# Batch 0 of an attention and MoE kernel by other routes: half of q and k by two more queues in fp32, v first, global keys by a one-hot matmul, masks on VectorE

## The chip, the cores and the metric

The kernel runs on one core of one Trainium2 chip. The metric is the device time of one execution in microseconds (us); smaller is better.

Engine names as in the profile: PE is the TensorE matmul, DVE is VectorE, ACT is ScalarE, POOL is GpSimd, SP is SyncE. A name with a `q` behind it (`SPq`) is that engine's sequencer issuing a DMA.

## The reference, cut to what matters

```python
batch, n_heads, seq, head_dim = (8, 8, 576, 64)      # q, k, v in fp32; n_global = 8
scores = (1/sqrt(D)) * q @ k.T
mask = abs(pos_i - pos_j) <= 32                      # a band of 65 keys ...
mask = mask | is_global[:, None] | is_global[None,:] # ... plus 8 global rows and columns
attn = softmax(where(mask, scores, -1e9)) @ v
x = attn.transpose(0, 2, 1, 3).reshape(4608, 512)
h = x @ w_in                                         # first layer, 512 x 2048
g = h + sin(alpha * h)**2 / (alpha + 1e-9)
out = g @ w_out                                      # second layer, 2048 x 512
```

## The kernel before

The 4608 tokens go through the two layers in nine chunks of 512. Chunk `p` holds the tokens that the attention of batch `p` has just finished, so the program is a pipeline: attention of batch 0 alone (the prologue), then first layer of chunk 0, then second layer of chunk 0 interleaved with the attention of batch 1, and so on. In the prologue the big matrix products have nothing to do. Data for the attention come in by three queues: GpSimd's (with a cast from fp32 to bf16 on the way), SP's and ACT's.

```python
# order of the prologue in the kernel before
zero_v(0); zero(Kps)                       # VectorE, two memsets of about 2.6 us among them
ld0 = load_slots(0, True)                  # GpSimd: cast loads of k, q by head, and of v
for f in ld0[:4]: f()                      # k, q of heads 0 and 1
...                                        # some 20 small GpSimd operations: the masks
for f in ld0[4:]: f()                      # v, then k, q of heads 2 to 7
for i, src in enumerate((k, q, v)):        # the 8 global rows of all 8 batches,
    for eng, js in halves:                 # half by SP, half by ScalarE; each DMA's address
        for j in js:                       # comes from a register that holds the index
            eng.dma_start(out=gN[i][j::NG], in_=src[:, :, bass.ds(regs[j], 1), :])
nc.scalar.dma_start(out=alphaT[:], in_=moe_alpha.rearrange("(t p) -> p t", p=P))
...                                        # masks on VectorE
stage_T(0, 0, psA, "qp")                   # transposes of k, q, heads 0 and 1
globals_all()                              # cast gN[0], gN[1] to gB; transposes into GT
...
globals_v_all()                            # VgN <- gN[2] (cast); recipT <- 1/alpha
shift_v(0); global_v(0)                    # SP: v shifted by half a window; VgN stored into VW
parts, last = attention(0, psA, {2: 0, 3: 2})
with_extra(parts, w_loads, 3, 2)           # GpSimd: w_in, w_out (four quarters each)
parts[3] = partial(chain, parts[3], pool_regs)
late = load_slots(1, True)                 # batch 1, issued inside chunk 0's first layer
```

A step of the attention is the scores (`Sp`), the exponential (`E`) times a mask, the denominators (`den`), and the value matmul (`num`), which reads `VW`: the window's rows of v, and at partitions 112 to 119 the global rows of v. These arrive by the longest path in the prologue: gather to `gN`, cast to `VgN`, then a store from SBUF to SBUF into `VW` (`VW<-VgN`). The outputs of global queries are scattered last, by eight register-addressed copies on GpSimd (`xT<-xg`); the first layer waits for those.

The softmax here doesn't subtract the row's maximum and nothing guards it: scores larger than these inputs give would overflow.

Of the kernel before, what the change touches and what calls it, by code (L numbers as in the profile page):

```python
# [18 lines left out]
def kernel(  # L19
# [12 lines left out]
    P = 128  # L32
# [99 lines left out]

    setup = tc.alloc_tile_pool(name="setup", bufs=1)
# [8 lines left out]
    nc.scalar.dma_start(out=gcol[KB : KB + NG, :], in_=global_idx[:, None])  # L142
    nc.scalar.preload_act_table_set("natural_log_exp_and_others")
# [4 lines left out]
    def zero_v(i):  # L148
        zero(VW[i][96:128].rearrange("p a u n -> p (a u n)").bitcast(F32))
        zero(VW[i][0:32, 0, 0, :].bitcast(F32))  # L150
        zero(VW[i][64:128, 1, NU - 1, :].bitcast(F32))

    zero_v(0)
    zero(Kps[:].bitcast(F32))

    ld0 = load_slots(0, True)
    for f in ld0[:4]:
        f()
    make_identity(nc, identb[:])


    MB = setup.tile([P, 3, QB], F32, name="MB")
    MG = setup.tile([P, NG], F32, name="MG")
    nc.gpsimd.memset(MB[:], 1.0)
    nc.gpsimd.memset(MG[:], 1.0)
    for base, cm, st_ in ((0, 1, -1), (2 * WIN, -1, 1)):
        nc.gpsimd.affine_select(
            out=MB[:], in_=MB[:], compare_op=ALU.is_ge, fill=0.0,
            base=base, channel_multiplier=cm, pattern=[[0, 3], [st_, QB]],
        )  # L170

    for i, base, cm in ((0, -WIN, 1), (2, S - 1 + WIN - (NW - 1) * QB, -1)):
        nc.gpsimd.affine_select(
            out=MB[:, i], in_=MB[:, i], compare_op=ALU.is_ge, fill=0.0,
            base=base, channel_multiplier=cm, pattern=[[0, QB]],
        )

    for base, cm in ((-WIN, 1), (WIN + QB - 1, -1)):
        nc.gpsimd.affine_select(
            out=MG[:], in_=MG[:], compare_op=ALU.is_ge, fill=0.0,  # L180
            base=base, channel_multiplier=cm, pattern=[[0, NG]],
        )

    RF = setup.tile([P, 1 + NG], F32, name="RF")
    nc.gpsimd.memset(RF[:], 1.0)
    for base, cm in ((-KB, 1), (KB + NG - 1, -1)):
        nc.gpsimd.affine_select(
            out=RF[:, 0:1], in_=RF[:, 0:1], compare_op=ALU.is_ge, fill=0.0,
            base=base, channel_multiplier=cm, pattern=[[0, 1]],
        )  # L190
    nc.gpsimd.affine_select(
        out=RF[:, 1:], in_=RF[:, 1:], compare_op=ALU.is_ge, fill=0.0,
        base=-KB - 1, channel_multiplier=1, pattern=[[-1, NG]],
    )
    IQi = setup.tile([P, S], DT.int32, name="IQi")
    nc.gpsimd.iota(IQi[:], pattern=[[1, S]], base=0, channel_multiplier=0)
    for f in ld0[4:]:
        f()

    for hp in range(NHP):  # L200
        zero(kTw[hp][:, :, KB:P])
    zero_v(1)
    nc.vector.memset(ones[:], 1.0)

    gN = [setup.tile([NG * B, DM], F32, name=f"gN{i}") for i in range(3)]
    halves = ((nc.sync, range(0, NG // 2)), (nc.scalar, range(NG // 2, NG)))
    regs = {}
    for eng, js in halves:
        for j in js:
            regs[j] = eng.value_load(  # L210
                gsc[0:1, 2 * j : 2 * j + 1], min_val=0, max_val=S - 1
            )
    for i, src in enumerate((k, q, v)):
        for eng, js in halves:
            for j in js:
                eng.dma_start(
                    out=gN[i][j : NG * B : NG, :].rearrange("b (h d) -> b h d", d=D),
                    in_=src[:, :, bass.ds(regs[j], 1), :].rearrange("b h o d -> b h (o d)"),
                )
    nc.scalar.dma_start(out=alphaT[:], in_=moe_alpha.rearrange("(t p) -> p t", p=P))  # L220

    Gf = setup.tile([P, NG], F32, name="Gf")
    nc.vector.tensor_copy(out=Gf[:], in_=gall[:].bitcast(DT.int32)[:, 0::2])
    Gp = setup.tile([P, 1], F32, name="Gp")
    nc.vector.tensor_copy(out=Gp[:], in_=gcol[:].bitcast(DT.int32)[:, 0:1])


    EQ = setup.tile([P, NG], F32, name="EQ")
    nc.vector.scalar_tensor_tensor(
        out=EQ[:], in0=Gf[:], scalar=Gp[:, 0:1], in1=RF[:, 1:],  # L230
        op0=ALU.is_equal, op1=ALU.mult,
    )
    flag = setup.tile([P, 1], F32, name="flag")
    nc.vector.tensor_reduce(out=flag[:], in_=EQ[:], axis=mybir.AxisListType.X, op=ALU.max)
    nc.vector.tensor_scalar(
        out=flag[:], in0=flag[:], scalar1=-1.0, scalar2=1.0, op0=ALU.mult, op1=ALU.add
    )
    nc.vector.tensor_tensor(out=flag[:], in0=flag[:], in1=RF[:, 0:1], op=ALU.mult)
    DQ = setup.tile([P, S], F32, name="DQ")
    nc.vector.tensor_copy(out=DQ[:], in_=IQi[:])  # L240
    nc.vector.tensor_scalar(
        out=DQ[:], in0=DQ[:], scalar1=Gp[:, 0:1], scalar2=None, op0=ALU.subtract
    )
    nc.vector.tensor_tensor(out=DQ[:], in0=DQ[:], in1=DQ[:], op=ALU.mult)
    nc.vector.tensor_scalar(
        out=DQ[:], in0=DQ[:], scalar1=float(WIN * WIN), scalar2=flag[:, 0:1],
        op0=ALU.is_gt, op1=ALU.mult,
    )
    DQv = DQ[:].rearrange("p (i c) -> p i c", c=QB)
# [305 lines left out]
    for p in range(NCH):  # L555
        fill = []
        late = []
        if p < B:
            with phase_pool("psA", 1) as psA:
                if p == 0:  # L560
                    stage_T(0, 0, psA, "qp")
                    globals_all()
                    for hp in range(NHP):
                        globals_in(0, hp, nc.vector)
# [94 lines left out]
```

## Time and profile before

The median is 386.33 us (385.18 to 386.82, three runs); the profiled run's span is 385.0 us. TensorE is busy for 87% of it.

From chunk 1 on TensorE has hardly a gap: about 38.4 us per chunk. So a change to the prologue is read in the timeline up to chunk 1's first layer. The columns are start, duration, engine, source line, operation, output and inputs, shapes, count; the bracket says how long the engine had been idle and what ended that.

```profile
11.51 3.99 ACTq L216 DMA_DIRECT2D gN<-in_v_dram  x4
...
20.42 0.81 SPq L127 DMA_DIRECT2D VW<-VgN  x1
...
22.03 0.73 ACT L342 ACTIVATE E<-Sp 128x672 bf16<-128x672 f32 x1
...
25.36 0.25 DVE L279 RECIPROCAL recipT<-alphaT 128x16 f32<-128x16 f32 x1 [4.96 <-DMA alphaT<-in_moe_alpha_dram]
...
29.27 0.58 PE L375 MATMUL num<-E,VW 128*64 128x56 bf16 x12 [2.36 <-DMA VW<-VgN]
...
46.29 16.56 PE L457 MATMUL hb<-xT,w_in 128*128 128x512 bf16 x64 [3.36 <-POOL xT L402]
62.69 1.89 PE L494 MATMUL ops<-w_out,H2b 128*128 128x512 bf16 x8
...
90.68 9.67 PE L457 MATMUL hb<-xT,w_in 128*128 128x512 bf16 x44 [1.46 <-POOL xT L402]
```

The reader is to see four milestones: first exponential 22.03, first value matmul 29.27 (it waits for the store of the global rows of v), first layer of chunk 0 at 46.29, lasting to the second layer's start at 62.69, and first layer of chunk 1 at 90.68.

### The profile page before, as it was taken

The page shows a single profiled execution, that of the slowest core. Times are in us where ns is not written, and L with a number is a line of the kernel's source. Part 1 is how long each engine was busy: PE and PEld are TensorE (multiplying, and loading weights), DVE is VectorE, ACT ScalarE, POOL GpSimd, SP SyncE. Part 2 cuts the span into 40 slices and gives each one's busy share as a digit, 9 for nine tenths or more (in the row PEclk, how much of TensorE's full clock was granted, in tenths as well). Part 3 has the DMA queues.
Part 4 walks back from the last instruction along what each step waited for, and adds up shares of the span by engine and source line. Part 5 has one row for each costly group of instructions (what it writes and reads, how often), then busy time and mean ns, then how long its engine had stood idle before and what let it go on. Part 6 is the DMA issues. An engine that isn't in the chain of part 4 may idle for free.

```text
span 385.0 us, 8609 instructions
## 1 busy us (share of the span) xinstructions
PE 336.2 (87%) x3208; PEld 162.9 (42%) x3208; DVE 244.9 (64%) x551; ACT 258.4 (67%) x435; POOL 249.3 (65%) x394
## 2 busy tenths in 40 slices
PE   1128499798999999999999999999999999999796
PEld 0015244443444444444544444444444444344342
DVE  7725459574977497649774976497749774954500
ACT  1057487786988588858885888578857885744310
POOL 8934396227878589858986898689768006854400
PEclk9999999999999999999999999999999999999989
DMA  6999999257999409940994099409940001000012
GB/s 53 136 162 161 190 164 165 37 77 77 155 132 153 124 9 103 148 127 7 103 148 126 7 103 149 128 6 113 137 128 5 30 30 54 2 28 27 29 54 82
DMA packets 133723, 35.31 MB, mean 92 GB/s; under 512 B 123314, under 2 KB 128178, under 8 KB 133682
## 3 DMA queue, kind: packets, MB, share of 16 engines
q0 software_dynamic: 122560, 19.02, 69.4%
q1 hardware_dynamic: 8034, 15.54, 13.9%
q10 hardware_dynamic: 3088, 0.21, 0.8%
q8 instruction: 25, 0.41, 0.4%
q14 instruction: 16, 0.13, 0.1%
HBM read 38.42 MB, written 9.44 MB: 124 GB/s over the span
## 4 chain that ended last, share of the span: by engine, by line
PE 52%; ACT 18%; DVE 10%; issue 7%; POOL 7%; DMA 3%; POOLq 1%; ACTq 0%; DVEq 0%
PE hb L457 22%; PE ops L494 13%; PE o L494 8%; ACT Sb L464 6%; ACT E L342 4%; DMA KS<-in_k_dram 3%; DVE H2b L447 3%; PE num L375 3%; ACT S L470 2%; DVE S L472 2%; DVE kTw L310 2%; ACT lnd L358 2%; PE hb L494 2%; ACT rec L360 2%; PE Sp L336 2%
## 5 line engine op out<-in xcount | busy, mean ns | idle before, releaser
L457 PE MATMUL hb<-xT,w_in 128*128 128x512 bf16 x576 | 133.1, 384 | 6.0 <-POOL xT L402 4.8
L464 ACT ACTIVATE Sb<-hb,alphaT 128x512 bf16<-128x512 f32 x144 | 96.6, 684 | 55.2 <-PE hb L457 53.9
L447 DVE SCALAR_TENSOR_TENSOR H2b<-S,recipT,hb 128x512 bf16<-128x512 bf16 x144 | 102.6, 741 | 29.3 <-POOL S L472 28.8
L472 POOL TENSOR_TENSOR S<-Sb 128x512 bf16<-128x512 bf16 x91 | 92.6, 1040 | 34.1 <-ACT Sb L464 31.5
L457 PEld LDWEIGHTS <-w_in 128*128 128x128 bf16 x576 | 56.5, 99 | 74.4 <-issue 10.9
L494 PE MATMUL ops<-w_out,H2b 128*128 128x512 bf16 x320 | 81.7, 385 | 3.2 <-DVE osb L502 3.0
L494 PEld LDWEIGHTS <-H2b 128*128 128x128 bf16 x576 | 50.6, 98 | 58.6 <-issue 7.3
L344 DVE TENSOR_TENSOR E<-E,MASK 128x672 bf16<-128x672 bf16 x64 | 34.1, 534 | 32.9 <-ACT E L342 32.2
L494 PE MATMUL o<-w_out,H2b 128*128 128x512 bf16 x224 | 54.7, 380 | 0.0
L342 ACT ACTIVATE E<-Sp 128x672 bf16<-128x672 f32 x64 | 45.9, 717 | 4.1 <-PE Sp L336 4.0
L402 POOL COPY xT<-xg 128x4 bf16 x64 | 12.9, 201 | 48.9 <-DVE xg L400 45.5
L107 POOL DMA_DIRECT2D VW<-in_v_dram x56 | 42.5, 776 | 0.7 <-issue 0.3
L358 ACT ACTIVATE lnd<-den 128x288 f32<-128x288 f32 x64 | 26.4, 412 | 18.3 <-PE den L352 17.8
L382 DVE TENSOR_TENSOR xT<-num,rec 128x288 bf16<-128x288 f32 x64 | 28.7, 449 | 6.1 <-PE num L375 4.8
L375 PEld LDWEIGHTS <-VW 128*64 128x64 bf16 x768 | 18.3, 116 | 33.1 <-DVE gn L386 10.9
L472 DVE TENSOR_TENSOR S<-Sb 128x512 bf16<-128x512 bf16 x30 | 18.3, 609 | 21.5 <-ACT Sb L464 20.6
L375 PE MATMUL num<-E,VW 128*64 128x56 bf16 x768 | 25.3, 201 | 6.9 <-DVE gn L386 3.1
L360 ACT ACTIVATE rec<-lnd 128x288 f32<-128x288 f32 x64 | 28.3, 443 | 2.0
L310 DVE COPY kTw<-Kps 128x1344 bf16<-128x1344 bf16 x32 | 27.1, 848 | 1.9 <-PE Kps L304 1.9
L336 PE MATMUL Sp<-qT,kTw 64*128 64x56 bf16 x768 | 22.1, 190 | 6.0 <-ACT E L342 4.1
L100 POOL DMA_DIRECT2D QS<-in_q_dram x30 | 23.2, 774 | 3.0 <-DMA QS<-in_q_dram 3.0
L324 ACT COPY qT<-qp 128x576 bf16<-128x576 bf16 x20 | 12.7, 633 | 18.4 <-PE ops L268 13.2
(73 smaller groups left out, 305.1 us busy)
## 6 DMA issues: line engine op xcount, KB each, us to landing
out_dram<-osb SPq DMA_DIRECT2D x36, 256.0 KB
VW<-in_v_dram POOLq DMA_DIRECT2D x40, 112.0 KB, 4.8
VW<-VW SPq DMA_DIRECT2D x8, 384.0 KB
KS<-in_k_dram POOLq DMA_DIRECT2D x30, 96.0 KB, 4.7
QS<-in_q_dram POOLq DMA_DIRECT2D x30, 96.0 KB, 4.7
w_in<-in_moe_w_in_dram POOLq DMA_DIRECT2D x4, 512.0 KB, 8.0
w_out<-in_moe_w_out_dram POOLq DMA_DIRECT2D x4, 512.0 KB, 13.1
VW<-VW SPq DMA_DIRECT2D x8, 240.0 KB
```

Of the source, the lines that this page charges most:

```text
L107: nc.gpsimd.dma_start(out=W[p0 : p0 + n, par, u, :].rearrange("p (h d) -> p h d", d=D), in_=v[b, :, key0 : key0 + n, :].rearrange("h p d - ...
L310: nc.vector.tensor_copy(out=kTw[hp][:, :, 0:KB], in_=bass.AP(tensor=base.tensor, offset=base.offset, ap=[list(base.ap[0]), [QB, NW], [1, KB]],
L342: nc.scalar.activation(out=E[:], in_=Sp[:, :, 0:EW], func=AF.Exp, scale=scale)
L344: nc.vector.tensor_tensor(out=E[:], in0=E[:], in1=mk[:, None, :].to_broadcast([P, 2, EW]), op=ALU.mult)
L358: nc.scalar.activation(out=lnd[:], in_=den[:, :, 0:QB], func=AF.Ln)
L360: nc.scalar.activation(out=rec[:], in_=lnd[:], func=AF.Exp, scale=-1.0)
L375: nc.tensor.matmul(out=num[pr, u, :], lhsT=W[:, i % 2, i // 2, c0 : c0 + 64], rhs=E[:, t, u * QC : (u + 1) * QC], start=True, stop=True, s ...
L447: nc.vector.scalar_tensor_tensor(out=H2b[:, n_, :], in0=s_[:], scalar=recipT[:, n_ : n_ + 1], in1=h_, op0=ALU.mult, op1=ALU.add,)
L457: nc.tensor.matmul(out=h2[:], lhsT=w_in[:, ci, nt * P : (nt + 1) * P], rhs=xT[:, ci, c * CH : (c + 1) * CH], start=(ci == 0), stop=(ci == ...
L464: nc.scalar.activation(out=Sb[:], in_=h2[:], func=AF.Sin, scale=alphaT[:, nt : nt + 1])
L472: eng.tensor_tensor(out=S2[:], in0=Sb[:], in1=Sb[:], op=ALU.mult)
L494: nc.tensor.matmul(out=ops[:], lhsT=H2b[:, nt, ts * P : (ts + 1) * P], rhs=w_out[:, nt, :], start=(nt == 0), stop=(nt == NT - 1),)
```

## The change

Its intent is to start the attention of batch 0 sooner. Heads 0 to 3 of q and k come in fp32 by SP's and ACT's queues, free at the start, and are cast on chip by VectorE and ScalarE; v goes first on GpSimd's queue; batch 0's global keys and queries are picked out of the loaded rows by a one-hot matmul, so the gathered global rows of k and q are needed only for batch 1 and later; the masks are made from iotas on VectorE. Around this the order of much else moves: alpha becomes the last load of SP, `VgN`'s cast and its store come inside the third step of the attention, half of the scatter goes to VectorE, batch 1's k and q are issued before w_out's quarters, and the transposes of the k and q globals stand inside chunk 0's first layer.

```diff
+    for h in range(H // 2):
+        for eng, src, dst in ((nc.sync, k, KF), (nc.scalar, q, QF)):
+            eng.dma_start(out=dst[:, :, h, :], in_=src[0, h].rearrange("(t p) d -> p t d", p=TW))
     ...
+    for f in v0: f()                       # v first on GpSimd, then heads 4 to 7
+    for f in kq0[8:]: f()
-    ...  # memsets and affine_selects for the masks on GpSimd
+    ...  # masks from iotas on VectorE, one-hot matrix OH
+    gather(nc.sync, 2, range(0, NG // 2))          # global rows of v: issued first,
+    gather(nc.scalar, 2, range(NG // 2, NG))       # ahead of ScalarE's first cast
+    shift_v(0)
     def globals_v_all():
         nc.vector.tensor_copy(out=VgN[:], in_=gN[2][:])
-        nc.vector.reciprocal(out=recipT[:], in_=alphaT[:])
+        global_v(0)
+        gather(nc.sync, 0, range(NG))
+        gather(nc.sync, 1, range(NG))
+        nc.sync.dma_start(out=alphaT[:], in_=moe_alpha.rearrange("(t p) -> p t", p=P))
     def pool_regs():                       # now also NG // 2 registers on VectorE
+    def prep0(hp, psA):                    # casts, transposes, picks by one-hot matmul
     ... # stage_G: the scatter of batch 0 half on VectorE
-                    globals_v_all(); shift_v(0); global_v(0)
-                    parts, last = attention(0, psA, {2: 0, 3: 2})
-                    with_extra(parts, w_loads, 3, 2)
-                    parts[3] = partial(chain, parts[3], pool_regs)
-                    late = load_slots(1, True)
+                    parts, last = attention(0, psA, {1: -2, 2: 0, 3: 2})
+                    parts[1] = partial(chain, parts[1], pool_regs)
+                    parts[2] = partial(chain, parts[2], globals_v_all)
+                    with_extra(parts, w_loads[:4] + kq1[:8], 4, 2)
+                    late = kq1[8:] + w_loads[4:6] + v1 + w_loads[6:]
     ...
+                m1[6] = partial(chain, m1[6], globals_all)    # casts and transposes of gN[0], gN[1]
-    sq_early = lambda nt: nc.vector if nt % 2 else nc.scalar
+    sq_early = lambda nt: sq_late(nt) if nt > 8 else nc.vector if nt % 2 else nc.scalar
```

The last line gives most squares of tiles 9 to 15 of chunk 0 to GpSimd. Other lines of the diff are left out. Chunk 1's squares go to GpSimd as well; batch 2's loads are issued in another order; and `tc.manual_schedule()` is entered ahead of the prologue and no longer after its set-up.

## The prediction

> **What bounds the kernel now.** From 106 us on, TensorE sets the pace (the timeline: 38.4 us per chunk, hardly a gap), and the change leaves that alone except for chunk 1's squares, which go from ScalarE/VectorE to GpSimd; chunk 1's first layer was already at TensorE's rate (64 matmuls in 15.5 us), so I give that nothing. What can move is the prologue: the first MoE matmul starts at 46.29 us. Its chain in the timeline: K heads 2-3, issued on GpSimd after the masks and all of v, land at 18.5; first exponential 22.0; VectorE stands 5.0 us in the reciprocal waiting for alpha (until 25.36); the first value matmul waits until 29.27 for the global rows of v (cast 20.4, stored 21.2, held up behind a shift whose packets the DMA view shows until 26); eight attention steps take 15 us; GpSimd's eight scatter copies take 2.1 us.
>
> **Removed.** Two 2.6 us memsets, about 20 small GpSimd operations ahead of v, eight cast loads (0.72 us of GpSimd issue each), the alpha wait, half of the scatter. The Trainium skill (DMA: Bandwidth & Descriptors, "SWDGE vs HWDGE vs iDMA") allows a cast only on GpSimd's DMAs; so the fp32 loads pay casts on chip: 96x768, about 0.85 us each (estimate from 0.64 us for 64x512), two on VectorE, two on ScalarE.
>
> **Estimated new prologue.** K, Q heads 0-1 land by about 6 us, but ScalarE first issues four gathers with register loads (1.1 us each, as in the trace), so its cast starts at about 9; transposes, one-hot picks, first exponential at 13.4 (before: 22.0). VectorE then carries masks (3 us), the second cast, four register loads (1.6 us), and casts the global v rows at about 22, no earlier than before. But v lands about 10, so the shift is over by then and the store lands at 25-26: first value matmul at about 25.5, 3.8 us earlier. Picks (12 small matmuls per head pair, about 0.9 us while cold) cost about 1 us in the steps; the shared scatter gives back 1. First MoE matmul at about 42.5: gain about 4 us of the roughly 9 us of earlier data.
>
> **Given back.** The k, q globals' transposes now stand inside chunk 0's first layer after its seventh tile. In the timeline VectorE is then about 2 us behind TensorE, and the two casts (0.64 us each) come after that, so TensorE should stand 2-3.5 us there. That may let its clock fall: the Trainium skill (TensorE: Matmul & The Clock Gate, Part 1) puts the cold state after an idle window of about 3.4 us; this trace has the first 12 matmuls of the layer at 0.43 us, later ones at 0.216. Against it, squares of tiles 9-15 leave ScalarE, so the layer's tail (4 us after TensorE's end) shortens by about 1 us. w_out's last quarters, issued after batch 1's v at about 53, should land just in time.
>
> **Prediction.** 381.0 us, range 373 to 388; faster by over 2%: 0.33, within 2%: 0.60, slower by over 2%: 0.07. I lean a little above my sum (about 2-3 us) because the removed waits may compound.
>
> **What would show it.** First exponential near 13 us, first value matmul 24-27, still waiting for the store of the global v rows; first MoE matmul 40-44; a TensorE gap of 2-3.5 us at the transposes of the globals; from batch 2 on, the same 38.4 us per chunk.
>
> **What would make it wrong.** Faster: the global rows arrive sooner, or the attention of batch 0 runs on a warm clock. Slower: fp32 loads (4608 packets of 256 B) delay v; alpha, now loaded last by SP, arrives after the first sine; GpSimd, loading until about 54 us, delays the squares of tiles 9-15; w_out arrives late.

## More of the kernel before

All runs that are compared here were fast: granted TensorE clock of 0.97 to 1.00 over the span.

The page's chain of waits (followed back from the last instruction, shares of the span) has little of the memory in it:

```profile
PE 52%; ACT 18%; DVE 10%; issue 7%; POOL 7%; DMA 3%; POOLq 1%; ACTq 0%; DVEq 0%
```

## The result

The changed kernel takes 399.41 us (397.35 to 401.78, four runs) against 385.75 us (384.30 to 386.82, four runs): slower, ratio 1.0348, 95% interval 1.0289 to 1.0407. A ratio here and below is the mean time of one kernel's fast runs over that of the other's fast runs of the same rounds, so it is not quite the ratio of the medians quoted. Executions over 1.5% slower than the fastest of the same kernel are left out of the means. All outputs are right. The profiled execution has a span of 395.6 us. The four runs lie in two groups, 397.35 and 397.43 us (granted clock 0.996), and 401.39 and 401.78 us (0.987 and 0.974); the profile is of the first group, and no trace shows where the other two lost their 4 us. The profile's chain of waits shows a memory share of 12% where before it was 3%:

```profile
PE 51%; DMA 12%; ACT 10%; issue 9%; DVE 9%; POOL 7%; POOLq 1%; ACTq 0%; DVEq 0%
```

The timeline of the kernel after:

```profile
6.93 7.76 ACTq L246 DMA_DIRECT2D gN<-in_v_dram  x4
14.74 0.83 ACT L320 CAST QS<-QF 96x768 bf16<-96x768 f32 x1 [7.74 <-DMA gN<-in_v_dram]
...
18.47 0.73 ACT L408 ACTIVATE E<-Sp 128x672 bf16<-128x672 f32 x1
...
27.01 0.21 DVE L427 TENSOR_REDUCE gd<-den 128x8 f32<-128x48 f32 x1 [3.15 <-issue]
...
27.55 0.49 DVE L300 CAST VgN<-gN 64x512 bf16<-64x512 f32 x1
...
28.07 0.81 SPq L127 DMA_DIRECT2D VW<-VgN  x1
29.08 10.98 SPq L246 DMA_DIRECT2D gN<-in_k_dram  x8
...
35.69 0.60 PE L441 MATMUL num<-E,VW 120*64 120x56 bf16 x12 [11.04 <-DMA VW<-VgN]
...
40.26 6.58 SPq L246 DMA_DIRECT2D gN<-in_q_dram  x8
...
51.31 0.81 DVE L469 COPY xT<-xg 128x4 bf16 x4
...
52.19 0.99 POOL L469 COPY xT<-xg 128x4 bf16 x4 [15.50 <-DVE xT L469]
...
53.23 8.82 PE L525 MATMUL hb<-xT,w_in 128*128 128x512 bf16 x28 [3.16 <-POOL xT L469]
...
64.45 0.62 PE L290 MATMUL ops<-identb,gB 64*128 64x64 bf16 x8 [2.40 <-DVE gB L288]
...
65.00 9.63 PE L525 MATMUL hb<-xT,w_in 128*128 128x512 bf16 x36
...
67.00 1.52 POOL L600 DMA_DIRECT2D w_out<-in_moe_w_out_dram  x2 [2.04 <-DMA w_out<-in_moe_w_out_dram]
...
74.47 1.89 PE L562 MATMUL ops<-w_out,H2b 128*128 128x512 bf16 x8
...
80.60 1.02 PE L562 MATMUL ops<-w_out,H2b 128*128 128x512 bf16 x4 [2.86 <-DMA w_out<-in_moe_w_out_dram]
...
103.85 9.66 PE L525 MATMUL hb<-xT,w_in 128*128 128x512 bf16 x44 [1.46 <-POOL xT L469]
```

The first exponential is 3.6 us earlier (18.47), and the first value matmul is 6.4 us later: TensorE stands 11.04 us before it, for the store of the global rows of v. The store itself took no longer than in the kernel before. There its issue ended at 21.23 and the value matmul began 8.0 us later (SP's queue was still moving packets of the shift until 26); here these are 28.88 and 6.8 us. So the 6.42 us are a store that was issued 7.65 us later and took 1.23 us less.

Split at the milestones, in us:

| stretch | before | after | difference |
|---|---|---|---|
| start to first value matmul | 29.27 | 35.69 | +6.42 |
| to chunk 0's first layer | 17.02 | 17.54 | +0.52 |
| chunk 0's first layer (to the start of the second) | 16.40 | 21.24 | +4.84 |
| second layer with batch 1's attention, to chunk 1's first layer | 27.99 | 29.38 | +1.39 |
| sum, at chunk 1's first layer | 90.68 | 103.85 | +13.17 |

Later chunks win back a part: the spans differ by 10.6 us. From chunk 1's first layer to the last chunk's, the kernel before takes 229.3 us and the kernel after 228.1. All variants of the changed kernel below are like it (227.5 to 228.4), so something that they all keep does this; which part of the change it is was not tried. The other 1.3 us lie behind the last chunk's start, in a stretch that scatters from 63.6 to 65.4 us between the variants.

In the first layer the loss is a stall with a consequence. TensorE stands 2.40 us at the transposes of `gB`, because VectorE casts `gB` only when it gets there. The view by windows shows what follows. Its columns are the window and its length, busy time (and instructions) of PE, PEld, DVE, ACT and POOL, then the granted TensorE clock, the DMA share and GB/s:

```profile
65.00:66.00 1.00, 1.00 (x7) 0.44 (x5) 0.42 (x1) 0.00 (x0) 0.00 (x0) 0.69 2.09 164
66.00:67.00 1.00, 1.00 (x4) 0.37 (x3) 0.00 (x0) 0.41 (x1) 0.01 (x1) 0.50 2.36 155
67.00:68.00 1.00, 1.00 (x3) 0.30 (x2) 0.69 (x2) 0.27 (x1) 1.00 (x2) 0.50 2.43 155
68.00:69.00 1.00, 1.00 (x4) 0.40 (x3) 1.00 (x3) 0.69 (x1) 0.51 (x1) 0.60 2.40 163
69.00:70.00 1.00, 1.00 (x7) 0.45 (x5) 0.70 (x2) 0.99 (x2) 0.00 (x0) 1.00 1.47 133
```

In the window of the stall itself (62 to 64 us) the granted clock was 1.00. After it the clock is halved for about 3.4 us: a window's time at half speed is (1 - clock) / 0.5, and the four windows from 65 to 69 us give 0.62 + 1 + 1 + 0.80 = 3.42 us. The Trainium skill ("TensorE: Matmul & The Clock Gate", Part 1) describes this state: after an idle window of about 3.4 us the array runs at half its clock, and it takes a busy window of about 3.4 us to leave it. The trace agrees with the second part; the idle stretch here was only 2.40 us. The clock fell about 3.3 us after the last matmul ahead of the stall (62.05 to about 65.4), with some 0.9 us of work in between. The length of a pause alone doesn't decide it: the wait of 2.86 us that ends at 80.60 left the clock at 1.00. (The view says 1.00 for 46 to 51 us of the kernel before as well, where matmuls start every 0.43 us, half their later rate; so it isn't read ahead of the first fall that it shows.) The loss adds up: 2.40 stall, 0.55 for the transposes (64.45 to 65.00), and about 1.7 for 3.4 us at half speed: 4.65 of the measured 4.84.

### The profile page after: what moved, and what is told of

Read it like the earlier page. It is cut to its first block, busy times and chain, and to the rows that moved or that the text cites. A ratio compares the mean times of both kernels' runs of the same rounds, so it can differ in the third digit from the quotient of the medians.

```text
span 395.6 us, 8735 instructions
## 1 busy us (share of the span) xinstructions
PE 336.9 (85%) x3256; PEld 164.9 (42%) x3256; DVE 241.2 (61%) x558; ACT 256.0 (65%) x431; POOL 254.8 (64%) x382
## 4 chain that ended last, share of the span: by engine, by line
PE 51%; DMA 12%; ACT 10%; issue 9%; DVE 9%; POOL 7%; POOLq 1%; ACTq 0%; DVEq 0%
PE hb L525 23%; PE ops L562 13%; PE o L562 7%; DMA w_out<-in_moe_w_out_dram 6%; ACT E L408 3%; DMA w_in<-in_moe_w_in_dram 2%; DVE S L540 2%; PE num L441 2%; DVE H2b L515 2%; DVE kTw L373 2%; DMA KS<-in_k_dram 2%; DMA VW<-in_v_dram 2%; ACT lnd L424 2%; ACT Sb L532 2%; PE hb L562 2%
## 5 line engine op out<-in xcount | busy, mean ns | idle before, releaser
L525 PE MATMUL hb<-xT,w_in 128*128 128x512 bf16 x576 | 134.8, 388 | 5.6 <-POOL xT L469 4.6
L532 ACT ACTIVATE Sb<-hb,alphaT 128x512 bf16<-128x512 f32 x144 | 97.8, 685 | 63.0 <-PE hb L525 60.7
L540 POOL TENSOR_TENSOR S<-Sb 128x512 bf16<-128x512 bf16 x109 | 110.8, 1039 | 40.3 <-ACT Sb L532 37.6
L562 PE MATMUL ops<-w_out,H2b 128*128 128x512 bf16 x320 | 80.4, 380 | 5.9 <-DVE osb L570 3.0
L410 DVE TENSOR_TENSOR E<-E,MASK 128x672 bf16<-128x672 bf16 x64 | 32.9, 516 | 32.1 <-ACT E L408 31.4
L441 PE MATMUL num<-E,VW 120*64 120x56 bf16 x768 | 25.3, 201 | 14.5 <-DMA VW<-VgN 11.0
L100 POOL DMA_DIRECT2D QS<-in_q_dram x42 | 32.6, 777 | 5.1 <-DMA w_in<-in_moe_w_in_dram 5.1
L441 PEld LDWEIGHTS <-VW 120*64 120x64 bf16 x768 | 18.5, 116 | 40.0 <-issue 18.3
L100 POOL DMA_DIRECT2D KS<-in_k_dram x42 | 33.0, 786 | 1.6 <-DMA w_in<-in_moe_w_in_dram 1.5
L540 DVE TENSOR_TENSOR S<-Sb 128x512 bf16<-128x512 bf16 x22 | 16.3, 740 | 19.3 <-ACT Sb L532 19.0
```

Of the source, the lines that this page charges most:

```text
L100: nc.gpsimd.dma_start(out=dst[:, t, :, :], in_=src[b, :, t * TW : (t + 1) * TW, :].rearrange("h p d -> p h d"),)
L410: nc.vector.tensor_tensor(out=E[:], in0=E[:], in1=mk[:, None, :].to_broadcast([P, 2, EW]), op=ALU.mult)
L441: nc.tensor.matmul(out=num[pr, u, :], lhsT=W[0 : KB + NG, i % 2, i // 2, c0 : c0 + 64], rhs=E[0 : KB + NG, t, u * QC : (u + 1) * QC], star ...
L525: nc.tensor.matmul(out=h2[:], lhsT=w_in[:, ci, nt * P : (nt + 1) * P], rhs=xT[:, ci, c * CH : (c + 1) * CH], start=(ci == 0), stop=(ci == ...
L532: nc.scalar.activation(out=Sb[:], in_=h2[:], func=AF.Sin, scale=alphaT[:, nt : nt + 1])
L540: eng.tensor_tensor(out=S2[:], in0=Sb[:], in1=Sb[:], op=ALU.mult)
```

## The experiments

The theory after the first look: (A) the store of the global rows of v is issued too late, behind ScalarE's gathers, VectorE's masks and four register loads; (B) when it is issued, it shares the DMA engines with w_in's cast loads, which GpSimd had begun at 20.93, and so takes 6.8 us from the end of its issue to the value matmul; (C) the casts of `gB` stall the first layer and cool the clock; (D) w_out is issued too late. Rivals: the casts on chip or the one-hot picks themselves cost the time, or one of A to D explains it alone.

Edits are against the kernel after, unless another one is named. Runs e1 to e4 were one call, and so were e5 to e8, e9 and e10, e11 and e12, e13 and e14, e15 and e16; e17 was alone. Each has its own runs of the kernel before in its ratio. All times stand in the table at the end of this section.

### e1: the casts of the k and q globals before the first layer

```diff
     def globals_all():
         for i in range(2):
-            nc.vector.tensor_copy(out=gB[i][:], in_=gN[i][:])
     ...
             if p == 0:
+                for i in range(2):
+                    nc.vector.tensor_copy(out=gB[i][:], in_=gN[i][:])
                 nc.vector.reciprocal(out=recipT[:], in_=alphaT[:])
```

> The changed kernel, with the two casts of the gathered k and q rows moved on VectorE to just before the first layer of chunk 0 (VectorE stands idle there for 5 us); the eight transposes stay after the seventh tile. Theory: chunk 0's first layer took 21.2 us instead of 16.4 because TensorE stood 2.4 us at those transposes and then ran cold again; without the wait it takes 16.5 to 17.5 us and the run is 3.5 to 4.5 us shorter than the changed kernel. Rival: the longer layer comes from GpSimd's late squares and loads; then the layer stays above 20 us and the time moves by less than 1 us.

400.23 us, not faster than after. The first layer did shrink, to about 18 us: the stall and the cold stretch were gone. But the second layer then waited for w_out as long as was won:

```profile
74.11 1.02 PE L561 MATMUL ops<-w_out,H2b 128*128 128x512 bf16 x4 [0.41 <-DMA w_out<-in_moe_w_out_dram]
...
80.88 1.86 PE L561 MATMUL ops<-w_out,H2b 128*128 128x512 bf16 x4 [5.74 <-DMA w_out<-in_moe_w_out_dram]
```

C and D hide each other: w_out lands at about 80.6 to 80.9 in both kernels, whatever TensorE does before. In e1 this longer wait also let the clock fall again; it was halved for 6.8 us from 79.4 on, in part while TensorE still stood.

### e2: no register loads on VectorE, the whole scatter on GpSimd

```diff
-        for eng, rs in ((nc.gpsimd, pregs), (nc.vector, vregs)):
-            for j in range(NG if eng is nc.gpsimd else NG // 2):
+        for j in range(NG):                # on GpSimd alone
     ...
-            eng, rs = (nc.vector, vregs) if b == 0 and j < NG // 2 else (nc.gpsimd, pregs)
+            # nc.gpsimd for all eight copies
```

> The changed kernel, with the scatter of batch 0 all on GpSimd as before, so VectorE loads no registers (3.15 us of it lie before the cast of the global v rows at 27.55). Theory A (the late cast alone sets the first value matmul): cast at about 24.4, store lands about 3 us earlier, first value matmul at about 32.5 instead of 35.7; scatter 0 to 1 us longer; run about 2 to 3 us shorter. Theory B (the store is held up by the w_in loads on the same DMA engines until they have drained, whenever it is issued): first value matmul stays at 34.5 to 35.7 and the run is within 1 us of the changed kernel.

399.65 us: no gain. The store was issued at 26.61 instead of 28.07, and still the value matmul began only at 34.48 instead of 35.69, 7.1 us after the end of the issue. Issuing sooner into the same traffic wins little, which speaks for B. The second wait for w_out grew to 4.62 us, and the clock fell there too (halved for 10.2 us).

### e3: the cast and the store of the global rows of v before the masks

```diff
                     prep0(0, psA)
+                    globals_v_all()
                     masks()
     ...
-                    parts[2] = partial(chain, parts[2], globals_v_all)
```

> The changed kernel, with the cast of the global v rows and its store issued right after the first head pair is prepared (VectorE at about 17, before the masks) and not after the third unit. The store then goes out at about 18, before w_in is issued at 20.9. Theory: the first value matmul waits for this store alone; it lands at about 22, and the first value matmul starts at 25 to 28, when its other inputs are ready: 8 to 10 us earlier than in the changed kernel, and the run is 8 to 10 us shorter. Rival: something else (the cold steps, the one-hot picks, the late q cast) holds the first value matmul; then it moves by less than 4 us.

393.56 us, ratio 1.0209 (1.0154 to 1.0264). The store is issued at 18.32, before w_in's first load; the first value matmul begins at 25.83 without waiting for it, and the first layer at 45.66. So A is right, and B is what makes lateness expensive. The 2.40 us at `gB` and the wait for w_out (3.39) are still there. The register loads show what they cost where they now stand: before the first sum of denominators VectorE stands 3.14 us, which the timeline puts down to issue alone.

```profile
18.32 0.81 SPq L127 DMA_DIRECT2D VW<-VgN  x1
...
25.83 0.53 PE L441 MATMUL num<-E,VW 120*64 120x56 bf16 x12
```

### e4: the store late, but w_in held until the first value matmul is done

```diff
+    def hold():                            # one small GpSimd copy that reads xT
+        held = const.tile([1, 8], BF, name="held")
+        nc.gpsimd.tensor_copy(out=held[:], in_=xT[0:1, 0, 0:8])
     ...
-                    with_extra(parts, w_loads[:4] + kq1[:8], 4, 2)
+                    with_extra(parts, [hold] + w_loads[:4] + kq1[:8], 4, 2)
```

> The changed kernel, with GpSimd held before w_in until the first unit of batch 0 is out (one extra 1x8 copy on GpSimd reads it), so no w_in and no batch 1 loads run while the global v rows are stored. Theory B (the w_in loads hold up the store, 28.9 issued, 35.7 landed): the store lands within 2 to 3 us and the first value matmul starts at 31 to 32.5. Theory A (the store is slow by itself): it still starts at 35 to 36. In both, the first layer may then wait for w_in, so the total time decides nothing here; the start of the first value matmul does.

397.25 us. This run measures B by itself (with w_in it also holds batch 1's loads, which stand behind w_in on GpSimd): the store is issued at the same time as in after, and lands in half the time, 3.2 us after the end of its issue instead of 6.8. With w_in under way the same interval is 6.8 us in e1, 7.1 in e2 and 7.0 in e10.

```profile
28.18 0.81 SPq L127 DMA_DIRECT2D VW<-VgN  x1
...
32.22 0.60 PE L445 MATMUL num<-E,VW 120*64 120x56 bf16 x12 [7.38 <-DMA VW<-VgN]
```

The view of the DMA queues, for the stretch from 28 to 32 us (queue, kind, then packets, MB and share of the 16 engines), says why. First the kernel after, then e4; q0 carries GpSimd's loads, q1 SP's (in e4 the store and the first gathers of k):

```profile
q0 software_dynamic: 824, 0.81, 123.0%
```

```profile
q1 hardware_dynamic: 246, 0.13, 25.0%
```

In after SP's queue moved no packet in these 4 us although its store was issued at 28.07; w_in's rows of about 1 KB filled the engines. The Trainium skill ("DMA: Bandwidth & Descriptors", "Queues, rings and completion order") says that each DMA engine goes round between the queues it has work for, packet by packet. These 4 us don't look like that: the store, once issued, moved no packet for over 3 us. Whether it had to wait for packets already handed out or for its own descriptors, and whether what the trace counts as a packet is a packet of the page, no run here tells apart.

### e5: e3, and all of w_out before batch 1's loads

```diff
-                    with_extra(parts, w_loads[:4] + kq1[:8], 4, 2)
-                    late = kq1[8:] + w_loads[4:6] + v1 + w_loads[6:]
+                    with_extra(parts, w_loads + kq1[:6], 4, 2)
+                    late = kq1[6:] + v1
```

> The run with the early global v rows (its median was 393.6), plus all four w_out loads issued on GpSimd directly after w_in, ahead of batch 1's k and q. There the first layer of chunk 1's phase still waited 3.4 us for the last w_out quarter. Theory: the late w_out is a limit of its own; the wait goes to 0 and the run is about 3 us shorter (390 to 391). Rival: the loads only change places on saturated DMA engines, something else arrives late (batch 1's k, q or v, or w_in for the first layer) and the time moves by less than 1 us.

391.79 us, ratio 1.0098 (1.0037 to 1.0159). No wait for w_out is left. The stall at `gB` is still there (3.60 us).

### e6: e5 with the casts of e1

> The previous one plus the casts of the gathered k and q rows before the first layer. Theory: with early casts alone the first layer shrank from 21.2 to 16.5 to 18 us but TensorE then stood 6.2 us for w_out, so nothing was won; with w_out early the same edit is worth 3.5 to 4.5 us: 386 to 387. Rival: the first layer's length does not matter even now; less than 1 us.

386.14 us, ratio 0.9970 (0.9914 to 1.0026). The loss is undone. The first layer takes 16.4 us (47.13 to 63.5), as before the change. The same edit that won nothing in e1 wins 5.7 us here against e5, because w_out is there in time. That is more than was expected: in e5 TensorE had stood 3.60 us, and the clock had been halved for 6.8 us.

### e7: e6 with the edit of e2

> The previous one without the four register loads of VectorE and with batch 0's scatter all on GpSimd. Theory: with the global v rows early, VectorE's 3.1 us of register loads stand directly before the second value matmul (it waited 2.2 us for VectorE), so now they cost 2 to 3 us, less up to 1 us for the scatter: 384 to 385. Rival: the halved scatter is worth as much as the loads cost; no change within 1 us.

384.95 us, ratio 0.9924 (0.9876 to 0.9971). The first value matmul is at 25.34 us, where the prediction had it (25.5), but chunk 0's first layer is only at 46.49: GpSimd, whose scatter stands in order behind its load issues, was held at one of them until 43.63, so that TensorE waited 6.84 us for the scatter. The interval of the ratio lies below 1; but chunk 1's first layer is no earlier than in the kernel before (91.14 against 90.68), and e9, one edit further, shows no gain, so this isn't read as one.

### e8: all gathers of v on SP, so that ScalarE can cast at once

```diff
-    gather(nc.sync, 2, range(0, NG // 2))
-    gather(nc.scalar, 2, range(NG // 2, NG))
+    gather(nc.sync, 2, range(NG))
     shift_v(0)
+    nc.sync.dma_start(out=alphaT[:], ...)  # from globals_v_all; against e7, VgN at step 2 again
```

> The previous one with all eight gathers of global v rows on SP (four were on ScalarE and held its first cast until 14.7), the cast of the global v rows back after the third unit, and alpha loaded before the gathers of k and q. Theory: ScalarE casts q at about 7, the first exponential comes at about 11 instead of 18.5, and the first value matmul at 21 to 24 instead of 25.8; the run is 2 to 4 us shorter, 380 to 383, faster than the kernel before. Rival: the store of the global v rows, the shift of v before it, or w_in set the start at 25 or later; no gain.

399.89 us. Half of it worked: without the gathers ScalarE's first cast came at 7.58 and the first exponential at 11.30, a little ahead of the prediction's 9 and 13.4, so those two steps of the prediction failed by the gathers, with the register loads among them. The other half broke by the edit itself: eight gathers kept SP until 19.7, and the store, directly behind alpha's 2048 elements of 4 bytes in SP's queue, took 7.54 us to issue and longer still to land.

```profile
7.58 0.83 ACT L317 CAST QS<-QF 96x768 bf16<-96x768 f32 x1 [0.49 <-DMA QF<-in_q_dram]
...
11.30 0.73 ACT L405 ACTIVATE E<-Sp 128x672 bf16<-128x672 f32 x1
...
22.81 7.54 SPq L127 DMA_DIRECT2D VW<-VgN  x1
...
41.83 0.60 PE L438 MATMUL num<-E,VW 120*64 120x56 bf16 x12 [24.27 <-DMA VW<-VgN]
```

### e9: e7 with four instead of six of batch 1's loads ahead of the scatter

> The run without VectorE's register loads, with two of batch 1's k and q loads moved from before batch 0's scatter to after it on GpSimd. There the scatter's input was ready at about 41 but GpSimd stood until 43.6 on the semaphore of a w_out load and TensorE waited 6.8 us for the scatter. Theory: the scatter starts at about 41, the first layer at about 43.3 instead of 46.5, and the run is 2.5 to 3.5 us shorter, about 382. Rival: the moved loads hold GpSimd's squares in the first layer, or the first layer then waits for w_in or alpha; gain under 1 us.

385.19 us, ratio 0.9997 (0.9956 to 1.0038). The scatter is no longer held: first layer at 43.66, 2.6 us earlier than before the change. The gain is then given back inside it: alpha, issued by SP at 37.62 behind 16 gathers, landed at 50.97, and the sine needs it.

```profile
50.97 0.69 ACT L529 ACTIVATE Sb<-hb,alphaT 128x512 bf16<-128x512 f32 x1 [9.56 <-DMA alphaT<-in_moe_alpha_dram]
```

### e10: e9 with ScalarE's gathers behind its first cast, and alpha between the gathers of k and q

```diff
-    gather(nc.scalar, 2, range(NG // 2, NG))
     ...
                     prep0(0, psA)
+                    gather(nc.scalar, 2, range(NG // 2, NG))
                     masks(); zero_v(1)
+                    globals_v_all()
```

> The previous one, with ScalarE's four gathers of global v rows moved behind its first cast and copies, the cast and store of the global v rows behind the masks, and alpha loaded between the gathers of k and of q. Theory: ScalarE's first cast moves from 14.9 to about 7.6 (as in the run with all gathers on SP), the first exponential to about 16, the first value matmul from 25.3 to 22 to 23.5, the run 1.5 to 3 us shorter: 379 to 381. Rival: the store of the global v rows now meets the w_in loads and lands 3 to 4 us later than it should (25 or later): no gain or a small loss.

388.20 us, ratio 1.0071 (1.0043 to 1.0100): worse than e9. ScalarE casts at 7.62, but its four gathers now stand between the cast and the first exponential and take it 8.40 us (10.77 to 19.17), so that this comes at 20.49. The store is issued at 21.83, meets w_in's loads as in after, and the first value matmul comes at 29.68.

### e11 and e12: alpha by rows

Alpha is read as 16 rows of 512 bytes and turned by a small fp32 matmul with an identity, instead of as 2048 elements of 4 bytes; e11 does it in e9, e12 in the kernel before.

```diff
-    nc.scalar.dma_start(out=alphaT[:], in_=moe_alpha.rearrange("(t p) -> p t", p=P))
+    nc.scalar.dma_start(out=alN[:], in_=moe_alpha.rearrange("(t p) -> t p", p=P))
     ...
+        nc.tensor.matmul(out=ps[:], lhsT=alN[:], rhs=idf[:], start=True, stop=True)
+        nc.vector.tensor_copy(out=alphaT[:], in_=ps[:])
```

> The run with the scatter ahead of the moved loads, with alpha loaded as 16 rows of 512 B early and turned on TensorE (one fp32 matmul with a 16x16 identity) in place of 2048 elements of 4 B loaded last. There the first layer began at 43.7 but its first sine waited until 51.0 for alpha (issued 37.6), and TensorE then stood 3.2 us. Theory: the sine follows the first tile (about 45.5), the layer takes 16.5 to 17.5 us, chunk 1's first layer starts at 88 to 89.5 instead of 92.6, and the run is 3 to 4 us shorter: 381 to 382.5, faster than the kernel before by about 1%. Rival: w_in, w_out or batch 1's loads then hold the layer or the next phase; gain under 1 us.

386.83 us, ratio 1.0031 (0.9998 to 1.0064). The first layer has its full pace (16.3 us), but it begins at 48.37: the store was issued at 20.49 instead of 18.32, and the turning costs TensorE a wait of 1.56 us in the middle of the attention. This run changed more than the packets, so it leaves the size of alpha's own part open.

> The kernel before, with the same alpha edit alone. Its VectorE stood 5.0 us for alpha (until 25.4), and 2048 packets of 4 B ran beside the shift of v that the global v rows' store queued behind. Theory: the small packets delayed shift and store; without them the first value matmul starts at 26 to 28 instead of 29.3 and the run is 1.5 to 3 us shorter than before: 383 to 384.5. Rival: shift and store are held by the loads of k and q heads and w_in; the first value matmul stays within 0.5 us of 29.3 and the time within 0.5 us.

389.32 us, ratio 1.0081 (1.0047 to 1.0116). In the kernel before, taking alpha's small packets and VectorE's 4.96 us of waiting away made nothing faster: k of heads 2 and 3 landed 2.0 us later (20.56 instead of 18.54), the store was issued at 22.45 instead of 20.42, and the first value matmul moved from 29.27 to 30.97. The rival, that something else than alpha's packets sets these times, holds in so far, though it had expected no change; why k landed later was not pursued. The trace of before agrees: VectorE went on at 25.36, and the value matmul had to wait for the store until 29.27 in any case. So that wait, which the prediction lists among what is removed, lay off the critical path.

### e13: e9 with alpha between the gathers of k and q

> The run with the scatter ahead of the moved loads, with alpha loaded by SP between the gathers of k rows and of q rows and not after both. Theory: alpha then lands before the first tile is done, the first layer starts at about 43.7, takes 16.5 to 18 us, and chunk 1's first layer starts at 88.5 to 90 (kernel before: 90.7): 382 to 384, 0.5 to 1% faster than before. Rival: alpha still lands after 47 or the q rows come late to their cast; then chunk 1's first layer starts at 91 or later and the time is that of the kernel before.

387.81 us, ratio 1.0031 (0.9987 to 1.0076). (VectorE's casts of the globals also move behind the reciprocal of alpha.) Alpha, issued 7.6 us earlier, lands only 4.4 us earlier, and the gathers of q, now behind it, take SP 15.94 us to issue instead of 6.58, so VectorE's casts of them hold the first layer:

```profile
31.11 15.94 SPq L246 DMA_DIRECT2D gN<-in_q_dram  x8
...
46.53 0.69 ACT L529 ACTIVATE Sb<-hb,alphaT 128x512 bf16<-128x512 f32 x1 [5.85 <-DMA alphaT<-in_moe_alpha_dram]
```

### e14: e13 with the first q cast on VectorE

```diff
-            nc.scalar.copy(out=QS[:, :, hs, :], in_=QF[:, :, hs, :])
+            if hp == 0:
+                nc.vector.tensor_copy(out=QS[:, :, hs, :], in_=QF[:, :, hs, :])
+            else:
+                nc.scalar.copy(out=QS[:, :, hs, :], in_=QF[:, :, hs, :])
```

(Two more copies of the same head pair go to VectorE as well, and `globals_v_all()` stands behind the masks.)

> The previous run, with the first head pair's q cast and its two copies on VectorE, which stood idle from 8 to 17, and the cast of the global v rows behind the masks. ScalarE's gathers then hold only the first exponential (about 16.5, from 18.5). Theory: the first value matmul moves from about 25.5 to 22 to 23.5 and the run is 1.5 to 3 us shorter than the previous one: 380 to 382. Rival: the store of the global v rows lands at 25 or later (behind the shift, beside w_in) and the gain is under 1 us.

387.94 us, ratio 1.0039 (1.0005 to 1.0073). The attention is the fastest so far: first value matmul at 22.84, first layer at 41.02, 5.3 us earlier than before the change. All of it is given back: the first sine waits 8.40 us for alpha, and VectorE, which casts the rows of q ahead of the layer's other work and gets them only at 52.91, lets TensorE stand.

```profile
54.38 1.86 PE L524 MATMUL hb<-xT,w_in 128*128 128x512 bf16 x4 [6.63 <-DVE H2b L514]
```

### e15 and e16: alpha out of the way, the casts of the globals late in the first layer

```diff
+        # e15: alpha directly behind the store, ahead of the gathers of k
+        # e16: alpha on ScalarE's queue, behind its four gathers of v
     ...
-                m1[6] = partial(chain, m1[6], globals_all)
+                m1[10] = partial(chain, m1[10], globals_cast)
+                m1[13] = partial(chain, m1[13], globals_all)      # transposes alone
```

> Same as e14, but alpha is issued directly behind the store of the global rows of v (about 19.4 us instead of 30.7), and the casts and transposes of the k and q globals stand at the eleventh and fourteenth tile of chunk 0's first layer instead of ahead of the layer and at the seventh tile. Theory (the start that e14 gained, 41.02 us against 46.29, was given back only because alpha landed at 46.9 and the q rows at 50): alpha lands by about 36, so the first sine waits less than 0.5 us, no TensorE gap over 1 us inside the first layer except up to 2 us at the late transposes, chunk 1's first layer starts at 88 or earlier (before 90.68, e14 92.93), total 379 to 383 us. Rival (what comes into the chip in this stretch is limited by the queues together, so that each transfer brought forward pushes another back): alpha early, but w_in or the q rows later; chunk 1's first layer again at 91 to 93, total 385 to 388 us.

386.10 us, ratio 0.9997 (0.9940 to 1.0055).

> Same as e15, but alpha is issued by ScalarE behind its four gathers of v (about 15 us), so it doesn't stand in SP's queue between the store and the k rows. Theory as for e15: first exponential 0.5 to 0.8 us later than in e14 (16.4), store of the v globals unchanged at about 22 us, alpha landed by about 32, no wait of the first sine, total 379 to 383 us. Rival: alpha's 4-byte packets slow the store or the shift, the first value matmul moves from 22.8 to 25 or later, total 385 to 388 us.

385.31 us, ratio 1.0005 (0.9944 to 1.0066). In both no wait for alpha or for the rows of q is left in the first layer, which starts at 41.32 and 41.73. By the time the rival was right, and by the trace neither was: chunk 1's first layer starts at 91.37 and 91.50 again, and the reason is a queue, not the memory. The lines of e16:

```profile
53.65 5.49 POOL L107 DMA_DIRECT2D VW<-in_v_dram  x7
59.16 5.03 POOL L543 TENSOR_TENSOR S<-Sb 128x512 bf16<-128x512 bf16 x5
...
60.24 0.69 ACT L535 ACTIVATE Sb<-hb,alphaT 128x512 bf16<-128x512 f32 x1 [3.24 <-POOL S L543]
...
61.04 1.87 PE L528 MATMUL hb<-xT,w_in 128*128 128x512 bf16 x4 [3.15 <-DVE H2b L518]
```

GpSimd issues the loads of batch 1 until 59.1 us, and only then comes to the five squares that the change gave it; TensorE waits 3.15 us at the end of the layer, and the clock is halved for 6.8 us from 60.0 on.

### e17: e16 with the squares of chunk 0 on VectorE and ScalarE in turn, as before the change

```diff
-    sq_early = lambda nt: sq_late(nt) if nt > 8 else nc.vector if nt % 2 else nc.scalar
+    sq_early = lambda nt: nc.vector if nt % 2 else nc.scalar
```

> Same as e16, but in chunk 0 the squares of tiles 9 to 15 run on VectorE and ScalarE in turn, as in before, instead of on GpSimd. In e15 and e16 no transfer holds the first layer any more, but GpSimd issues the loads of batch 1 until 59.1 us and begins the five squares only then (59.16 to 64.2); ScalarE waits 3.24 us and TensorE 3.15 us for that. Theory (that is the last thing that gives the early start back): first layer from about 41.7 to 57.5 us without a gap over 1 us, last H2b by about 61 instead of 66.4, chunk 1's first layer at 86 to 88 (before 90.68), total 379 to 382 us. Rival (something else in the chunk-1 phase, the loads of batches 1 and 2 or w_out, arrives at a fixed time): the second layer starts early and then waits; chunk 1's first layer stays at 90 to 92, total 384 to 387 us.

382.88 us (379.82 to 383.34, six runs) against 385.64 (eleven runs): ratio 0.9903, 95% interval 0.9863 to 0.9942. This is the first variant whose early start survives: it beats the kernel before by about 1%, which counts as the same at 2%. Not all of that is the early start. Of the 4.1 us between the profiled spans, 2.9 lie ahead of chunk 1's first layer and 1.5 in the chunks behind it, where all variants of the changed kernel are faster than the kernel before; the last stretch gives 0.3 back.

```profile
43.91 13.70 PE L528 MATMUL hb<-xT,w_in 128*128 128x512 bf16 x53 [0.22 <-issue]
...
57.63 0.62 PE L294 MATMUL ops<-identb,gB 64*128 64x64 bf16 x8
58.18 1.90 PE L528 MATMUL hb<-xT,w_in 128*128 128x512 bf16 x8
...
60.93 1.89 PE L565 MATMUL ops<-w_out,H2b 128*128 128x512 bf16 x8 [0.86 <-DVE GT L299]
...
87.80 9.66 PE L528 MATMUL hb<-xT,w_in 128*128 128x512 bf16 x43 [1.46 <-POOL xT L472]
```

The first layer has no gap at the transposes, the second follows with 0.86 us of waiting, and chunk 1's first layer starts at 87.80, 2.9 us ahead of before. The times fit the theory except that this run's attention was 1.4 us slower than e16's (first layer at 43.10, with the same program up to there), and the total of 382.88 lies just above the 379 to 382 that the theory gave.

### All runs

Milestones are from the profiled run of each, in us; one trace each. e16 and e17 are the same program up to the first layer and differ there by 1.4 us, so differences below about 1.5 us between traces are not read.

| run | median us | ratio to before (95%) | first value matmul | chunk 0's first layer | chunk 1's first layer |
|---|---|---|---|---|---|
| before | 385.75 | 1 | 29.27 | 46.29 | 90.68 |
| after | 399.41 | 1.0348 (1.0289 to 1.0407) | 35.69 | 53.23 | 103.85 |
| e1 | 400.23 | 1.0364 (1.0299 to 1.0428) | 35.60 | 53.43 | 105.42 |
| e2 | 399.65 | 1.0333 (1.0272 to 1.0395) | 34.48 | 52.22 | 106.15 |
| e3 | 393.56 | 1.0209 (1.0154 to 1.0264) | 25.83 | 45.66 | 97.17 |
| e4 | 397.25 | 1.0274 (1.0216 to 1.0331) | 32.22 | 50.58 | 102.62 |
| e5 | 391.79 | 1.0098 (1.0037 to 1.0159) | 25.98 | 46.22 | 97.54 |
| e6 | 386.14 | 0.9970 (0.9914 to 1.0026) | 27.00 | 47.13 | 91.23 |
| e7 | 384.95 | 0.9924 (0.9876 to 0.9971) | 25.34 | 46.49 | 91.14 |
| e8 | 399.89 | 1.0305 (1.0241 to 1.0368) | 41.83 | 59.84 | 104.81 |
| e9 | 385.19 | 0.9997 (0.9956 to 1.0038) | 25.83 | 43.66 | 92.64 |
| e10 | 388.20 | 1.0071 (1.0043 to 1.0100) | 29.68 | 47.45 | 92.79 |
| e11 | 386.83 | 1.0031 (0.9998 to 1.0064) | 28.27 | 48.37 | 92.44 |
| e12 | 389.32 | 1.0081 (1.0047 to 1.0116) | 30.97 | 49.96 | 94.51 |
| e13 | 387.81 | 1.0031 (0.9987 to 1.0076) | 25.11 | 42.80 | 92.22 |
| e14 | 387.94 | 1.0039 (1.0005 to 1.0073) | 22.84 | 41.02 | 92.93 |
| e15 | 386.10 | 0.9997 (0.9940 to 1.0055) | 23.51 | 41.32 | 91.37 |
| e16 | 385.31 | 1.0005 (0.9944 to 1.0066) | 23.97 | 41.73 | 91.50 |
| e17 | 382.88 | 0.9903 (0.9863 to 0.9942) | 25.34 | 43.10 | 87.80 |

From e6 to e16, leaving out e8 and e12, the start of chunk 0's first layer varies between 41 and 48 us while chunk 1's stays at 91 to 93. Until e17 each variant had some other thing that arrived at a fixed time.

## Why the prediction was wrong

The prediction gave 381.0 us, the result was 399.41, outside its range and on the side to which it gave 0.07.

1. "its cast starts at about 9" and "first exponential at 13.4": failed. The cast came at 14.74 and the exponential at 18.47. The gathers of v were costed "with register loads (1.1 us each, as in the trace)". But the four in that trace took 3.99 us with their registers loaded beforehand; in the change each loads its own, and the four took ScalarE 7.76 us. SP's gathers of k show both kinds in one trace: the first four find their registers loaded and start 0.82 us apart (29.08 to 31.55), the last four load one each and start 1.97 us apart (33.48 to 39.40). So a register load costs about 1.1 us there, an estimate from these starts. e8, without gathers on ScalarE, had 7.58 and 11.30. The mechanism was right; the term "four gathers" was mis-sized by 3.4 to 3.8 us, and they began only at 6.93.
2. "four register loads (1.6 us), and casts the global v rows at about 22": failed. The loads cost 3.15 us, and with the exponential being late the cast came at 27.55.
3. "the store lands at 25-26: first value matmul at about 25.5": this is the step that failed most, by 10 us. Besides 1 and 2, it took for granted that the store, with the shift over, meets an idle memory. GpSimd had begun w_in's four loads at 20.93, seven microseconds before the store was issued, and e4 shows what that costs: 6.8 against 3.2 us. Of the 10.2 us, 5.5 are the later cast (27.55 instead of 22) and 4.6 the longer way from the cast to the value matmul (8.1 us instead of 3.5). The prediction named only the fp32 loads as what might be in v's way. With the store ahead of w_in (e3, e7) the first value matmul came at 25.83 and 25.34, so the number was within reach of the change's parts, in another order.
4. "the shared scatter gives back 1": it gave about 0.2 us. The two halves write one tile, and GpSimd's copies began at 52.19, just after VectorE's had ended (51.31 to 52.12). They ran one behind the other. Picks "about 1 us in the steps": about 0.7 measured, right.
5. "TensorE should stand 2-3.5 us there. That may let its clock fall": right, 2.40 us, and the clock fell to half for 3.4 us. The prediction put its cost at no definite number; measured, the layer grew by 4.84 us.
6. "w_out's last quarters, issued ... at about 53, should land just in time": failed. GpSimd issued them at 67.00, after it had stood 2.04 us until an earlier quarter of w_out had landed, and TensorE waited 2.86 us at 80.60. e1 shows the real size: with the stall at `gB` gone it is 5.74 us.
7. "I lean a little above my sum ... because the removed waits may compound": the opposite. The removed waits did not compound, the added ones did: C and D hid each other in e1, and three further items (scatter behind loads in e7, alpha and the rows of q in e9 to e14, squares behind loads in e15 and e16) came out one after another. Of the removed ones the wait for alpha had lain off the critical path (the trace of before, and e12).
8. Among what "would make it wrong" the prediction listed alpha arriving after the first sine, w_out late, and GpSimd delaying the squares of tiles 9 to 15. All three occurred, w_out in after itself, the other two only once the attention was fast enough to meet them. They were listed as risks and given a chance of 0.07 together, although each of them was an order on one queue that could have been counted in advance.
9. "from batch 2 on, the same 38.4 us per chunk": nearly. The chunks of the kernel after take 37.96 to 38.23 us, those of the kernel before 37.97 to 38.48; the 1.3 us that this saves had no term in the prediction.

What is shown and what is not: A, C and D are shown by undoing them (e3, e6 with e1, e5), B by e4. B makes a late store dear; a loss against the kernel before it is not, since the store took 8.0 us there. The casts and picks as such are not the cause, since e17 keeps them (with the first q cast on VectorE) and is faster than before. That e3's whole gain of about 5 us belongs to the store, and none to the 16 gathers and alpha that moved with it, was not separated. Nor was each of the edits in e17 tried alone, so e17's 1% belongs to their sum, and the faster later chunks to a part of the change that nobody isolated.

## What to carry to other kernels

Before giving work to idle queues and engines at the start, write down for each engine the order of everything it issues, and for each small transfer on the critical path what large transfers are already under way when it is issued; a store of 96 KB that is issued behind two megabytes of weights pays double. When a stall is removed and the time doesn't move, look for the next thing that arrives at a fixed time: in this kernel w_out, alpha, gathered rows and GpSimd's squares each hid behind the one before, and only the sum of the edits paid. An engine that issues loads in order is a poor place for compute that others wait for.

## What the Trainium skill lacked or had wrong

- "TensorE: Matmul & The Clock Gate", Part 1, puts the fall of the clock after an idle window of about 3.4 us. Here 2.40 us of idleness was enough in two kernels (after and e3): the granted clock was 0.50 afterwards, for about 3.4 us. A pause of 2.86 us in after and one of 3.39 us in e3 left it at 1.00. The page's figure for the way back agrees: the other falls measured here last twice 3.4 us (e1, e5, e16) or three times (e2's second).
- "DMA: Bandwidth & Descriptors", "Queues, rings and completion order", has the engines go round between queues at packet granularity. In after SP's queue moved no packet from 28 to 32 us while 824 packets of GpSimd's queue went through, with a store on it since 28.07; the store took 6.8 us against 3.2 without that traffic. That doesn't show the page wrong; it has no figure for such a small transfer beside a stream of cast loads.
- No page was found to say what a load of 4-byte elements does to the issues behind it on the same queue: directly after alpha's 2048 elements the next issue on SP took 7.54 us instead of 0.81 (e8), and eight gathers took 15.94 us instead of 6.58 (e13); in e15, where alpha went ahead of most of the weights, the eight gathers behind it took 12.84 us against 11.45 without it (e9).
- No page was found with the cost of loading an index register from SBUF; the nearest is a floor of about 600 ns for a `tensor_load` ("DMA: Bandwidth & Descriptors", "Latency and other measured facts"). Here it was about 0.79 us each on VectorE (four in 3.15 us, with nothing else issued) and about 1.1 us each among SP's gathers, an estimate from starts 1.97 and 0.82 us apart; four gathers with their register loads took ScalarE 7.76 us.
